# A recurrent attention kernel: the next mask matmul behind the token AV, one PSUM pool, later gates in the MLP, and w1 in three loads

**Chip, cores, metric.** One core of one Trainium2 chip. The metric is the device time of one execution in microseconds (us).

## The reference

The output is `g * a + (1 - g) * b`. Here `a` is an attention over 64 segments of 32 tokens that carries 8 memory rows from each segment to the next, and `b` is an MLP. Cut to what matters:

```python
def _A_ref(x, mem0, Wq, Wk, Wv, Wo, seg_len):      # S = 2048, Dm = 512, H = 32, Dh = 128, M = 8, seg = 32
    mem = mem0
    for s in range(n_seg):
        h = concat([mem, x[:, s*seg:(s+1)*seg]])      # 40 rows
        q, k, v = h @ Wq, h @ Wk, h @ Wv
        p = softmax(where(mask, q @ k.T * scale, -1e9))
        o = (p @ v) @ Wo
        mem = o[:, :M]                                # what the next segment waits for
        outs.append(o[:, M:])
def _B_ref(x, w1, b1, w2, b2):                     # F = 1376
    return gelu(layernorm(x) @ w1 + b1) @ w2 + b2
g = sigmoid((x * gate_w).sum(-1, keepdims=True))
```

## The kernel before

The MLP runs first, then the loop over the segments, called iterations below. The token outputs of a segment are finished one iteration late (`av_x(s - 1)`); the memory rows cannot wait. The eight PSUM banks go by number: 0 to 4 rotate, 5 and 6 serve the filling work (`run_fill`: matmuls that other segments need), and bank 7 (`B`) holds the scores, the mask, later the sums `sr`, and the next memory rows `aT`. Names used below: AV is the matmul of the probabilities with V; `wsb` is the bf16 copy that ScalarE makes (casts) of the result of Wo; the memory matmul (`mem_out`) picks the memory rows out of `wsb`; `hT` is the transposed input of the next iteration, which waits for these rows.

```python
    mps = mlp.enter_context(tc.tile_pool(name="mps", bufs=1, space=PSUM))          # MLP: tp, hp, bp
    pools = {"ps": mlp.enter_context(tc.tile_pool(name="pre", bufs=1, space=PSUM)), "sb": mwork}
    ...
    nc.sync.dma_start(w1_sb[:, :, 0:3 * P], w1_src[:, :, 0:3 * P])
    ...                                             # x rows of tiles 2 and 3, first part of w2
    nc.sync.dma_start(w1_sb[:, :, 3 * P:F], w1_src[:, :, 3 * P:F])
    ...                                             # rest of w2, then x rows of tiles 4 to 7
    def mask_mm():
        B = bank(7, [P, 512])                       # four matmuls of 448 columns into bank 7
        ...
    mlp.close()                                     # end of the MLP: its pools close
    pb = loop.enter_context(tc.tile_pool(name="pb", bufs=1, space=PSUM))           # the loop's pool
    S_next = mask_mm()
    for s in range(nseg):
        T, si = divmod(s, SPT)                      # SPT = 4: si = s mod 4
        ...                                         # q, k, v, scores, exp, memory AV
        sums(sr, E[:, :, 16:48], True, False)       # sr lies in bank 7
        ...
        nc.vector.reciprocal(out=R[:, 8 * NG:].rearrange("p (i q) -> p i q", q=32), in_=sr)
        run_fill(1)
        for u in range(8):
            wo_unit(wp, UTT[Tp % 2], 24 - 8 * sp, u)           # 8 x 4 matmuls with Wo
        nc.scalar.copy(out=wsb[:], in_=wp[:])                  # the cast of wsb
        S_next = mask_mm()
        if s >= 1:
            av_x(s - 1, (nd, ne, na, nc_))                     # token AV: 40 matmuls
        run_fill(2 * (si == 3))
        if s + 1 < nseg:
            mem_out(aT, wsb)                                   # the memory matmul, 16 pieces
            nc.vector.tensor_copy(out=hn[:, :, 0:M], in_=aT)   # hT of the next iteration
        for _ in fill:
            pass
```

## Time and profile before

| | before |
|---|---|
| time, median of 4 runs | 820.96 us (820.43 to 822.13) |
| span of the profiled run | 820.2 us |
| head (loads), MLP, loop | 0 to 25, 25 to 99.5, 100 to 820 us |
| period of an iteration, median by s mod 4 = 0, 1, 2, 3 | 10.96, 10.77, 10.94, 11.44 us |
| idle TensorE at 12.57, 17.93, 25.05, 100.62 us | 1.36, 0.63, 1.52, 0.78 us |

Such a page is read from the top: the shares say which engine to look at, the chain says whether that engine is what the end waits for, and the timeline of one iteration says what it pauses for. Below, "from the last Wo" means: counted from the start of the last four of the 32 Wo matmuls of an iteration. This is the clock by which iterations are compared, and it comes from the trace's records of single instructions, which the views merge.

### The profile page before, as it was taken

Reading aid. Unit: us, or ns where it says so; the run is one execution under the profiler, and the core shown is the slowest. Engines: PE = TensorE matmul, PEld = TensorE weight load, DVE = VectorE, ACT = ScalarE, POOL = GpSimd, SP = SyncE. Lnnn points to the kernel's source line nnn. Section 1 sums busy time; section 2 is a strip of 40 time slices with the busy share of each in tenths; the row PEclk is TensorE's granted clock in tenths of the full one; section 3 lists DMA queues with packets and bytes.
Section 4 is the critical chain, followed back from the end, with each engine's and each line's share of the span. In section 5 each row is a group of like instructions: output and inputs, shape, how many; then the busy total and the mean of one; then the engine's idle time right before and its main releaser. Section 6 shows DMA issues by size and latency. Waiting matters only on the chain.

```text
span 820.2 us, 48440 instructions
## 1 busy us (share of the span) xinstructions
PE 791.7 (97%) x22013; PEld 443.6 (54%) x22013; DVE 473.6 (58%) x897; ACT 461.8 (56%) x1365; POOL 271.4 (33%) x623
## 2 busy tenths in 40 slices
PE   5999999999999999999999999999999999999986
PEld 3666555555555555555555555555555555555543
DVE  5764256565656656665656565656656565656554
ACT  3555455656565565555555655555655556565553
POOL 8100234242434243243424242433333242424220
PEclk9999999999999999999999999999999999999999
DMA  8791310000000010101010100000010101010000
GB/s 313 241 404 48 104 34 6 25 15 17 24 22 24 14 33 10 37 11 35 5 38 9 31 16 22 25 19 28 10 36 11 36 7 38 5 34 8 10 5 24
DMA packets 38357, 37.59 MB, mean 46 GB/s; under 512 B 13561, under 2 KB 36578, under 8 KB 36610
## 3 DMA queue, kind: packets, MB, share of 16 engines
q1 hardware_dynamic: 38018, 34.31, 12.5%
q8 instruction: 174, 2.85, 1.4%
q14 instruction: 37, 0.30, 0.1%
q0 software_dynamic: 128, 0.13, 0.1%
HBM read 26.03 MB, written 6.29 MB: 39 GB/s over the span
## 4 chain that ended last, share of the span: by engine, by line
PE 93%; DVE 2%; DMA 1%; SPq 1%; issue 1%; ACT 1%; DVEq 0%; ACTq 0%
PE b L211 34%; PE b L233 17%; PE b L222 17%; PE b L398 5%; PE hp L470 4%; PE bp L487 4%; PE b L360 3%; PE b L374 2%; PE b L383 2%; PE b L365 2%; PE b L403 1%; DMA Wo_sb<-in_A_x_dram 1%; PE b L387 0%; DVE R L692 0%; DVE hT L721 0%
## 5 line engine op out<-in xcount | busy, mean ns | idle before, releaser
L217 DVE STREAM_TRANSPOSE Tt<-b 128x512 f32<-128x512 f32 (+1 forms) x384 | 225.5, 613 | 78.9 <-PE b L211 67.0
L211 PEld LDWEIGHTS <-hT 128*32 128x32 bf16 x5120 | 131.3, 97 | 109.3 <-DVE hT L721 24.7
L233 PE MATMUL b<-Wo_sb,UTT 128*32 128x512 bf16 (+1 forms) x2656 | 160.9, 378 | 0.4
L222 PE MATMUL b<-Wv_sb,hT 128*32 128x512 bf16 x2048 | 141.8, 378 | 0.0
L704 DVE RECIPROCAL R<-b 128x256 f32<-128x256 f32 x63 | 110.7, 1757 | 49.3 <-ACT UTT L703 46.8
L211 PE MATMUL b<-Wq_sb,hT 128*32 128x512 bf16 x2048 | 133.3, 380 | 3.3 <-DVE hT L721 1.7
L211 PE MATMUL b<-Wk_sb,hT 128*32 128x256 bf16 (+1 forms) x3072 | 133.3, 308 | 0.0
L667 ACT CAST KT<-Tt 128x256 bf16<-128x256 f32 (+1 forms) x192 | 87.0, 476 | 53.3 <-DVE Tt L217 53.2
L620 POOL TENSOR_TENSOR Px<-E,R 128x256 bf16<-128x256 bf16 x63 | 42.5, 675 | 209.7 <-DVE R L704 209.7
L667 POOL CAST QT<-Tt 128x512 bf16<-128x512 f32 x64 | 39.1, 611 | 187.9 <-DVE Tt L217 187.9
L233 PEld LDWEIGHTS <-UTT 128*32 128x32 bf16 x2656 | 64.8, 96 | 61.2 <-ACT UTT L703 11.1
L711 ACT CAST wsb<-b 128x512 bf16<-128x512 f32 x63 | 36.9, 585 | 97.7 <-PE b L233 97.7
L634 ACT CAST UTT<-b 128x256 bf16<-128x256 f32 x248 | 74.5, 387 | 12.2 <-PE b L403 7.9
L692 DVE RECIPROCAL R<-b 128x64 f32<-128x64 f32 x63 | 35.1, 557 | 79.8 <-PE b L360 79.8
L667 ACT CAST QT<-Tt 128x512 bf16<-128x512 f32 x64 | 39.6, 619 | 66.1 <-DVE Tt L217 66.1
L703 ACT CAST UTT<-b 128x64 bf16<-128x64 f32 x252 | 35.3, 227 | 63.1 <-PE b L403 63.1
L222 PEld LDWEIGHTS <-hT 128*32 128x32 bf16 x2048 | 49.4, 96 | 21.2
L475 ACT ACTIVATE hg<-hp,b_sb 128x256 bf16<-128x256 f32 x80 | 37.7, 473 | 39.4 <-PE hp L470 39.4
L398 PEld LDWEIGHTS <-V 32*128 32x128 bf16 x4064 | 34.4, 91 | 45.0 <-DVE Pm L695 31.7
L721 DVE CAST hT<-b 128x32 bf16<-128x32 f32 x63 | 12.0, 191 | 79.8 <-PE b L365 79.8
L470 PE MATMUL hp<-yT,w_sb 128*128 128x256 bf16 (+1 forms) x352 | 53.8, 278 | 3.4 <-ACT hg L475 1.5
L622 POOL TENSOR_TENSOR racc<-racc,R 128x320 f32<-128x320 f32 x63 | 54.7, 868 | 0.0
(130 smaller groups left out, 1032.2 us busy)
## 6 DMA issues: line engine op xcount, KB each, us to landing
Wv_sb<-in_A_Wv_dram SPq DMA_DIRECT2D x4, 1024.0 KB
Wq_sb<-in_A_Wq_dram SPq DMA_DIRECT2D x4, 1024.0 KB
Wk_sb<-in_A_Wk_dram SPq DMA_DIRECT2D x4, 1024.0 KB
Wo_sb<-in_A_Wo_dram SPq DMA_DIRECT2D x2, 2048.0 KB
vd<-vt SPq DMA_DIRECT2D x32, 128.0 KB
vs<-vd SPq DMA_DIRECT2D x256, 16.0 KB
out_dram<-o SPq DMA_DIRECT2D x15, 128.0 KB
Wo_sb<-in_A_x_dram SPq DMA_DIRECT2D x1, 1024.0 KB
```

The source lines that it names most:

```text
L211: nc.tensor.matmul(bk[32 * j:32 * j + 32, 0:n], lhsT=G[:, kc, :], rhs=W5[t][:, kc, h0:h1, j, :], start=(kc == 0), stop=(kc == KC - 1), til ...
L217: nc.vector.transpose(out=Tt[:, 0:n], in_=bk[:, 0:n])
L222: nc.tensor.matmul(bk[32 * j:32 * j + 32, :], lhsT=G[:, kc, :], rhs=Wv5[:, kc, 4 * vb:4 * vb + 4, j, :], start=(kc == 0), stop=(kc == KC - ...
L233: nc.tensor.matmul(bk[32 * g:32 * g + 32, :], lhsT=ut[:, i, j, c0:c0 + 32], rhs=Wo_sb[:, 4 * i + j, d0:d1], start=(j == 0 and i < 4), stop ...
L398: nc.tensor.matmul(U[j][:, i, :], lhsT=V[q, i, :], rhs=Pt[q, i, c_main:c_main + n], start=(i == 0), stop=False, skip_group_check=True, til ...
L470: nc.tensor.matmul(hp[:rows, :], lhsT=w1_sb[:, kc, fc * P:fc * P + rows], rhs=yTs[blk][:, kc, :], start=(kc == 0), stop=(kc == KC - 1))
L475: nc.scalar.activation(out=hg_[:rows, :], in_=hp[:rows, :], func=ACTF.Gelu_apprx_tanh, bias=b1_sb[:rows, fc:fc + 1], scale=1.0)
L620: nc.gpsimd.tensor_tensor(out=Px[:, :, 0:32], in0=E[:, :, 16:48], in1=Rr, op=ALU.mult)
L622: nc.gpsimd.tensor_tensor(out=racc[:], in0=racc[:], in1=R[:], op=ALU.add)
L634: nc.scalar.copy(out=UTT[T % 2][:, :, j, c0 + M:c0 + 40], in_=U[:])
L667: (nc.gpsimd.tensor_copy if bi == 2 else nc.scalar.copy)(out=dst, in_=Tv)
L704: nc.vector.reciprocal(out=R[:, 8 * NG:].rearrange("p (i q) -> p i q", q=32), in_=sr)
```

## The change

The intent: the mask matmul writes bank 7, which the reciprocal still reads, so it should not stand first in TensorE's queue. A single PSUM pool removes the handover of banks between the MLP and the loop. Norms (the layernorm of rows of x) should not stand behind gates (the sums for `g`) on VectorE, and w1 should arrive in smaller pieces.

```diff
+    pb = loop.enter_context(tc.tile_pool(name="pb", bufs=1, space=PSUM))     # ahead of the MLP
-    mps = mlp.enter_context(tc.tile_pool(name="mps", bufs=1, space=PSUM))
...
-    nc.sync.dma_start(w1_sb[:, :, 3 * P:F], w1_src[:, :, 3 * P:F])
+    nc.sync.dma_start(w1_sb[:, :, 3 * P:6 * P], w1_src[:, :, 3 * P:6 * P])
+    nc.sync.dma_start(w1_sb[:, :, 6 * P:F], w1_src[:, :, 6 * P:F])
...
-        tp = mps.tile([P, KC, P], BF16, tag="tp", name="tp")
+        tp = bank(k, [P, KC, P], BF16)               # k = 7; 6 for the second transpose
-        hp = mps.tile([P, TB * P], FP32, tag="hp", bufs=2, name="hp")
+        hp = bank(u % 2, [P, TB * P])
-                bpt[T] = mps.tile([P, Dm], FP32, tag=f"bp{T % 4}", name="bp")
+                bpt[T] = bank((2, 3, 4, 6)[T % 4], [P, Dm])
...
-        elif fc in (2, 4, 6, 8):
-            T = T1 + (fc - 2) // 2
+        elif fc >= 7:
+            T = T1 + fc - 7
...                                                   # (other gates likewise)
-        S_next = mask_mm()
         if s >= 1:
             av_x(s - 1, (nd, ne, na, nc_))
         run_fill(2 * (si == 3))
+        S_next = mask_mm()
```

More of the change, by code (lines that the diff above doesn't have):

```diff
@@ L93 @@
     warm = mlpw.tile([P, 1], FP32)
-    mps = mlp.enter_context(tc.tile_pool(name="mps", bufs=1, space=PSUM))
-    pools = {"ps": mlp.enter_context(tc.tile_pool(name="pre", bufs=1, space=PSUM)), "sb": mwork}
+    pools = {"sb": mwork}
     man = tc.manual_schedule()
@@ L178, in bank @@
     def bank(k, shape, dtype=FP32):
-        return pools["ps"].tile(shape, dtype, tag=f"b{k}", name=f"b{k}")
+        return pb.tile(shape, dtype, tag=f"b{k}", name=f"b{k}")
     side_n, side_todo = [0], set()
@@ L453, in norm, with norm_tr @@
         return y_sb
-    def norm_tr(T, y_sb):
+    def norm_tr(T, y_sb, k=7):
         blk, tt = divmod(T, TB)
-        tp = mps.tile([P, KC, P], BF16, tag="tp", name="tp")
+        tp = bank(k, [P, KC, P], BF16)
         for kc in range(KC):
@@ L534 @@
     norm_tr(0, ys[0])
-    norm_tr(1, ys[1])
+    norm_tr(1, ys[1], 6)
     bn(2)
@@ L558 @@
                 newton(T1 + 2, T1 + 6)
-        elif fc in (2, 4, 6, 8):
-            T = T1 + (fc - 2) // 2
+        elif fc >= 7:
+            T = T1 + fc - 7
             if T < NT:
                 gates(T, T + 1)
-        elif fc == 10 and T1 < NT:
-            gates2(T1, T1 + 4)
+        if blk % 2 == 0 and blk > 0 and fc == 1:
+            gates2(TB * blk, TB * blk + 4)
         if blk == 0 and fc in (9, 10):
@@ L569 @@
             gates2(0, 2)
-        if blk == 1 and fc in (1, 3):
-            gates(2 + fc // 2, 3 + fc // 2)
+        if blk == 1 and fc in (5, 6):
+            gates(fc - 3, fc - 2)
         if blk == 1 and fc == 9:
@@ L594 @@
     racc = lp.tile([P, NG * 40], FP32)
-    pb = loop.enter_context(tc.tile_pool(name="pb", bufs=1, space=PSUM))
     cw = loop.enter_context(tc.tile_pool(name="cw", bufs=2))
-    pools.update(ps=pb, sb=cw, nTt=3, nside=2)
+    pools.update(sb=cw, nTt=3, nside=2)
     man = tc.manual_schedule()
```

## The prediction

> **What bounds the kernel now.** I read the page first (engine shares, chain), then the waits, then the timeline of single iterations, and last the single records behind it.
>
> ```profile
> PE 791.7 (97%) x22013; PEld 443.6 (54%) x22013; DVE 473.6 (58%) x897; ACT 461.8 (56%) x1365; POOL 271.4 (33%) x623
> PE 93%; DVE 2%; DMA 1%; SPq 1%; issue 1%; ACT 1%; DVEq 0%; ACTq 0%
> ```
>
> TensorE is busy 97% of the span and holds 93% of the chain that ended last; no other engine passes 58%. The kernel has three stages: a head that waits for loads (0 to 25 us), an MLP (25 to 99.5 us, in which TensorE shows no idle piece at all in the timeline), and 64 recurrent iterations of some 11 us each (100 to 820 us). What TensorE has to do is the same in both kernels, so only its pauses can be gained. The loop is 88% of the time, so its pauses count most. Here is the end of one iteration whose number s has s mod 4 = 2, and of the next, with s mod 4 = 3:
>
> ```profile
> 307.35 1.76 DVE L704 RECIPROCAL R<-b 128x256 f32<-128x256 f32 x1 [0.66 <-ACT UTT L703]
> 309.16 0.37 PE L374 MATMUL b<-MkA,ident 128*32 128x448 bf16 x4
> 309.26 0.58 ACT L711 CAST wsb<-b 128x512 bf16<-128x512 f32 x1 [1.67 <-PE b L233]
> 309.90 0.27 PE L365 MATMUL b<-Sel,wsb 128*32 128x8 bf16 x16
> ...
> 318.39 1.76 DVE L704 RECIPROCAL R<-b 128x256 f32<-128x256 f32 x1 [0.98 <-ACT UTT L703]
> 320.20 0.37 PE L374 MATMUL b<-MkA,ident 128*32 128x448 bf16 x4
> 320.31 0.58 ACT L711 CAST wsb<-b 128x512 bf16<-128x512 f32 x1 [1.67 <-PE b L233]
> 320.51 0.37 PE L398 MATMUL b<-Px,V 32*128 32x32 bf16 x32
> 320.89 0.61 PE L233 MATMUL b<-Wo_sb,UTT 128*32 128x512 bf16 x8
> 321.34 0.26 PE L365 MATMUL b<-Sel,wsb 128*32 128x8 bf16 x16
> ```
>
> Two things are to be seen. First, the mask matmul (L374) starts 0.05 us after the reciprocal (L704) ends, both times: it writes bank 7, which the reciprocal is reading, and so it waits. In the single records this is 53 to 55 ns in all 63 iterations that have it. Second, what the next iteration waits for is the memory matmul (L365). In the first iteration it starts at 309.90, and the cast of wsb (L711) ends at 309.26 + 0.58 = 309.84; in the single records L365 starts 53 or 54 ns after the end of that cast in all iterations but those with s mod 4 = 3 (and in s = 3). With s mod 4 = 3 the cast ended at 320.89 and L365 came only at 321.34, because eight more matmuls (L233, the filling work) stand before it.
>
> **What the Trainium skill says.** "PSUM — Partial Sum Buffer", section "PSUM bank collisions raise a hardware error", gives the rule to guard PSUM by bank, not by address. The trace agrees: the mask matmul waits for a reader of its bank until 53 ns after its end. "TensorE: Matmul & The Clock Gate", section "Wait — 56ns, not 53.3ns?", gives 215.7 ns from start to start for 512 columns on a warm array; the records show 0.216 us for each four of the L233 matmuls (four column tiles side by side). "TensorEngine Tiling (Array Packing)", section "Key Properties", says that a change of the tiling mode drains TensorE. The records show 0.306 us from a mask matmul (128x32 tiles) to the first L398 (32x128 tiles), where 448 columns alone would take some 0.19. The change keeps the number of such switches. "DMA: Bandwidth & Descriptors", section "Why small descriptors are slow (HBM only)", tells of a fixed cost of each packet and descriptor; the trace's packets are used below.
>
> **Part 1, the mask matmul behind the token AV (loop).** Nothing is added or removed on TensorE; the mask goes behind 40 AV matmuls, and where there is filling work, behind that too. Times from the start of the last four Wo matmuls, from single records of before:
> - s mod 4 = 3, before: mask at 0.327 (it could have gone at 0.216, had the bank been free), first AV at 0.632, last AV at 0.908, filling work 0.109 later, two times 0.216 for it, L365 at 1.458.
> - The same, after: first AV at about 0.333 (0.306 plus 27 ns for 64 more columns), last AV 0.276 later (0.609), filling work at 0.718, end of it at 1.150, mask 0.19, L365 at about 1.34. The gain is 0.12 us.
> - 13 such iterations (11, 15, ... 59), and s = 7 with one four of filling work (1.244 before, 1.12 after): 14 x 0.12 = **1.7 us**. The way from L365 to the next iteration (sum, cast hT, first L211: 0.6 us) is unchanged and on the path, so this gain stays.
> - The other iterations, before: L365 at 1.069, which is 0.431 to the start of the cast, 0.585 of the cast, 0.053 to L365. After: last AV 0.609, mode switch 0.16, mask 0.19, so TensorE is ready for L365 at 0.96. The cast still ends last, at 1.069. **Gain 0** in 49 iterations: TensorE waits 0.11 us in front of L365 in place of the wait in front of the mask.
>
> **Part 2, one PSUM pool.** Before, the loop's pool takes over banks of pools that close, and its first mask matmul waits for the last readers of them:
>
> ```profile
> 99.25 0.60 PE L487 MATMUL bp<-w_sb,hgl 97*128 97x512 bf16 x2
> 99.88 0.69 ACT L495 ACTIVATE c_all<-bp,omg_all 128x512 bf16<-128x512 f32 x1 [0.83 <-PE bp L487]
> 100.62 0.37 PE L374 MATMUL b<-MkA,ident 128*32 128x448 bf16 x4 [0.78 <-ACT c_all L495]
> ```
>
> The listing of the instructions' order, built for both, shows that the two waits before this matmul (on VectorE and on ScalarE) are gone. Its bank 7 was last used for a transpose in block 6, and the first banks of the loop (0 to 3) were freed earlier; bank 4, which the last c_all reads, comes fifth. TensorE then goes on at about 99.7 instead of 100.62: **0.9 us**. ScalarE still has c_all (to 100.57) and a table load of 1.28 us to do, so the first QT cast can start at 102.1, where 101.9 would be wanted; the pauses of ScalarE between the next casts (0.57 us) take that up.
>
> **Part 3, w1 in three loads, and a second bank for the first transposes (head).**
>
> ```profile
> 12.57 0.61 PE L470 MATMUL hp<-yT,w_sb 128*128 128x256 bf16 x4 [1.36 <-DMA w_sb<-in_B_w_dram]
> 16.34 0.69 DVE L413 BATCH_NORM_STATS2 st<-Wo_sb 128x6 f32<-128x512 bf16 x1 [3.36 <-DMA Wo_sb<-in_A_x_dram]
> 17.93 0.38 PE L459 MATMUL tp<-ident,y 128*128 128x128 bf16 x4 [0.63 <-DVE yT L460]
> 24.43 0.20 ACT L441 ACTIVATE th_all<-z_all 128x2 f32<-128x2 f32 x1 [2.50 <-DVE junk L438]
> 25.05 0.60 PE L470 MATMUL hp<-yT,w_sb 128*128 128x256 bf16 x4 [1.52 <-ACT hg L475]
> ```
>
> The wait of 1.36 us at 12.57 goes, and the first L470 comes 0.68 us earlier (at 6.24 to 7.34 the second yT copy waits for the second use of one bank). But VectorE stands idle 3.36 us for the x rows of tiles 4 to 7, which land at 16.3 behind all of w1 and w2, and from there runs without a pause (statistics, Newton steps, two gates) until the tanh at 24.43 frees ScalarE and TensorE. TensorE's early start ends in a longer wait at the transpose of 17.93 and at 25.05. So the head gains nothing, and the third load costs: the DMA's packet records give 82 ns for 1984 bytes (512 packets on 16 engines: 2.6 us), and 45 ns for 768 bytes and some 56 ns for 1216 (estimated between 49 at 1024 and 82 at 1984): 1.4 + 1.8 = 3.2 us; by medians 0.3 us more instead of 0.6. Estimate: **0.4 us lost**.
>
> **Part 4, gates of the MLP later in odd blocks.** Fourteen gate passes (0.75 us of VectorE each) move behind norms and transposes. TensorE shows no idle piece between 25.65 and 100.6 us, so there is nothing to win: **0 us**. The tanh that waits for them moves to the second step of the even block, about 4.3 us (five steps of 0.87) after the first of four gates, which take 3 us: no new wait expected.
>
> **Sum.** 821.4 - 1.7 - 0.9 + 0.4 = 819.2 us.
>
> **The rivals.** (a) The mask's wait is on the path in all iterations: 63 times 0.12 to 0.3 us (the waits view has 15.2 us of idle weight loads at L374, 63 times), which gives 802 to 814. Against it: the 53 ns from the wsb cast to L365. (b) The head gains what it no longer waits for, 1.4 to 2 us: about 817. Against it: the idle VectorE at 16.34. (c) New waits: a tanh in front of a gelu that has to wait for late gates, or an array that has cooled in a pause of 3 us near 15 to 18; each up to 1 us, about 820.5 to 821.5. (d) Single stalls move: iterations 9, 14 and 47 of before are 0.5 us longer than their like for no cause that the trace names, and half of those with s mod 4 = 0 are 0.13 longer. A shifted stream may lose or gain some 1.5 us.
>
> **Range and chances.** My sum is -2.2; (b) and (d) stretch it to -4.7, (c) and (d) to about 0, and before itself spread 1.7 us over three runs. So 816.8 to 821.8. Two per cent is 16 us: only (a) at its most would reach it, and I give it 1%; slower by 2% has no mechanism here, 1%.
>
> **What would show it.** L374 in the loop no longer starts at the reciprocal's end; L365 still starts 53 ns after the cast of wsb except with s mod 4 = 3, where the period falls from 11.44 to 11.32 us; the others stay at 10.77 to 10.95. The first mask matmul follows L487 at once. The wait at 12.57 is gone and that at 17.93 is longer, with 25.05 at 25.3 to 25.6. It is wrong if L365 comes earlier with s mod 4 below 3, if the end of the MLP moves by more than 0.7 us, or if TensorE shows new pauses between 25 and 99 us.

## The result, and the profile after

The changed kernel takes 816.83 us (median of 4 runs, 816.19 to 818.16) against 820.96 us. The ratio is 0.995, 95% interval 0.9932 to 0.9968. This is the same within 2%, and at the lowest edge of the range of 816.8 to 821.8: the forecast gain was 2.2 us (from 821.4, the median of the runs of before that the author then had), and the measured one is about 4.1.

The page of the kernel after shows the same bound:

```profile
PE 788.6 (97%) x22013; PEld 437.1 (54%) x22013; DVE 474.9 (58%) x897; ACT 455.7 (56%) x1365; POOL 272.0 (33%) x623
PE 93%; DVE 2%; DMA 1%; SPq 1%; ACT 1%; issue 1%; DVEq 0%; ACTq 0%
```

The loop, in the timeline of the kernel after: the same two iterations as in the prediction (line numbers have moved: L376 is the mask, L367 the memory matmul, L705 the reciprocal, L712 the cast of wsb, L400 the AV, L235 the filling work):

```profile
304.81 1.76 DVE L705 RECIPROCAL R<-b 128x256 f32<-128x256 f32 x1 [0.66 <-ACT UTT L704]
306.60 0.37 PE L400 MATMUL b<-Px,V 32*128 32x32 bf16 x32
306.71 0.58 ACT L712 CAST wsb<-b 128x512 bf16<-128x512 f32 x1 [1.67 <-PE b L235]
306.98 0.37 PE L376 MATMUL b<-MkA,ident 128*32 128x448 bf16 x4
307.35 0.27 PE L367 MATMUL b<-Sel,wsb 128*32 128x8 bf16 x16
...
317.75 0.59 ACT L712 CAST wsb<-b 128x512 bf16<-128x512 f32 x1 [1.67 <-PE b L235]
318.02 0.61 PE L235 MATMUL b<-Wo_sb,UTT 128*32 128x512 bf16 x8
318.46 0.36 PE L376 MATMUL b<-MkA,ident 128*32 128x448 bf16 x4
318.65 0.25 PE L367 MATMUL b<-Sel,wsb 128*32 128x8 bf16 x16
```

The mask no longer meets the reciprocal, which ended at 306.57. With s mod 4 = 2 the memory matmul starts at 307.35, still just behind the end of the cast of wsb (306.71 + 0.58 = 307.29). With s mod 4 = 3 it comes 0.90 us after the start of the cast, where it came 1.03 us after it before (320.31 to 321.34).

The waits view shows the exchange. First a line of it for the kernel before, then one for the kernel after (waiter, releaser, us in total, times, longest):

```profile
PEld L374 <- issue: 15.2, 63, 0.3
```

```profile
PEld L367 <- ACT wsb L712: 13.9, 50, 0.6
```

63 pauses of weight loads in front of the mask became 50 pauses in front of the memory matmul.

The way from the MLP to the loop, in the timeline of the kernel after:

```profile
99.24 0.60 PE L489 MATMUL b<-w_sb,hgl 97*128 97x512 bf16 x2
99.77 0.37 PE L376 MATMUL b<-MkA,ident 128*32 128x448 bf16 x4
99.87 0.69 ACT L497 ACTIVATE c_all<-b,omg_all 128x512 bf16<-128x512 f32 x1 [0.83 <-PE b L489]
```

The mask matmul is at 99.77 instead of 100.62, ahead of the c_all (the MLP's share of the output, written by ScalarE) it used to wait for. And the head, in the same timeline:

```profile
10.91 0.61 PE L472 MATMUL b<-yT,w_sb 128*128 128x256 bf16 x4 [0.30 <-DMA w_sb<-in_B_w_dram]
16.29 0.69 DVE L415 BATCH_NORM_STATS2 st<-Wo_sb 128x6 f32<-128x512 bf16 x1 [3.63 <-DMA Wo_sb<-in_A_x_dram]
17.89 0.38 PE L461 MATMUL b<-ident,y 128*128 128x128 bf16 x4 [1.78 <-DVE yT L462]
25.04 0.60 PE L472 MATMUL b<-yT,w_sb 128*128 128x256 bf16 x4 [1.56 <-ACT hg L477]
```

The wait for w1 fell from 1.36 to 0.30 us, the one near 17.9 grew from 0.63 to 1.78, and the piece at 25.05 us is at 25.04. One pair of profiles says little of the head, though: over all 14 profiles VectorE takes up the x rows (the line at 16.29) at 15.75 to 16.34 us in the six with w1 in two loads (mean 16.06) and at 16.11 to 16.46 in the eight with three (mean 16.21).

Where the 3.8 us between the two profiled spans (820.2 and 816.4) came from, by periods and single records of these two profiles:

| part | predicted | measured |
|---|---|---|
| 14 iterations with s mod 4 = 3 and filling work, from the last Wo to the next q | -1.7 | -1.8 |
| 16 iterations with s mod 4 = 0, the same stretch | 0 | **-1.3** |
| the other iterations, and the stretch from q to the last Wo (single stalls that come and go) | 0 | +0.3 |
| MLP to loop | -0.9 | -0.8 |
| head | **+0.4** | 0.0 |
| after the loop | 0 | -0.1 |

The +0.3 is a sum of -0.9 and +1.2: single stalls of up to 0.7 us fell in other places. The -1.3 us was not predicted, and the experiments had to find its cause. In the kernel before, 8 of the 16 iterations with s mod 4 = 0 take 0.13 to 0.22 us longer from the last Wo to hT than the rest. In the changed kernel's first profile none does.

### The profile page after: what moved, and what is told of

Its sections match the earlier page's. It is cut to its first block, busy times and chain, and to the rows that moved or that the text cites. A ratio compares the mean times of both kernels' runs of the same rounds, so it can differ in the third digit from the quotient of the medians.

```text
span 816.4 us, 48441 instructions
## 1 busy us (share of the span) xinstructions
PE 788.6 (97%) x22013; PEld 437.1 (54%) x22013; DVE 474.9 (58%) x897; ACT 455.7 (56%) x1365; POOL 272.0 (33%) x623
## 4 chain that ended last, share of the span: by engine, by line
PE 93%; DVE 2%; DMA 1%; SPq 1%; ACT 1%; issue 1%; DVEq 0%; ACTq 0%
PE b L213 34%; PE b L235 17%; PE b L224 16%; PE b L400 5%; PE b L472 4%; PE b L489 4%; PE b L362 3%; PE b L376 2%; PE b L367 2%; PE b L385 2%; PE b L405 1%; DMA Wo_sb<-in_A_x_dram 1%; PE b L389 0%; DVE hT L722 0%; PE b L322 0%
## 5 line engine op out<-in xcount | busy, mean ns | idle before, releaser
L235 PE MATMUL b<-Wo_sb,UTT 128*32 128x512 bf16 (+1 forms) x2656 | 161.8, 378 | 0.4
L705 DVE RECIPROCAL R<-b 128x256 f32<-128x256 f32 x63 | 110.7, 1758 | 49.2 <-ACT UTT L704 48.4
L235 PEld LDWEIGHTS <-UTT 128*32 128x32 bf16 x2656 | 64.8, 96 | 61.1 <-ACT UTT L704 11.1
L712 ACT CAST wsb<-b 128x512 bf16<-128x512 f32 x63 | 36.9, 585 | 97.7 <-PE b L235 97.7
L400 PEld LDWEIGHTS <-V 32*128 32x128 bf16 x4064 | 34.4, 91 | 59.4 <-DVE Pm L696 32.2
L477 ACT ACTIVATE hg<-b,b_sb 128x256 bf16<-128x256 f32 x80 | 37.7, 473 | 39.3 <-PE b L472 39.3
L472 PE MATMUL b<-yT,w_sb 128*128 128x256 bf16 (+1 forms) x352 | 53.8, 278 | 2.4 <-ACT hg L477 1.6
```

The source lines that it names most:

```text
L235: nc.tensor.matmul(bk[32 * g:32 * g + 32, :], lhsT=ut[:, i, j, c0:c0 + 32], rhs=Wo_sb[:, 4 * i + j, d0:d1], start=(j == 0 and i < 4), stop ...
L400: nc.tensor.matmul(U[j][:, i, :], lhsT=V[q, i, :], rhs=Pt[q, i, c_main:c_main + n], start=(i == 0), stop=False, skip_group_check=True, til ...
L472: nc.tensor.matmul(hp[:rows, :], lhsT=w1_sb[:, kc, fc * P:fc * P + rows], rhs=yTs[blk][:, kc, :], start=(kc == 0), stop=(kc == KC - 1))
L477: nc.scalar.activation(out=hg_[:rows, :], in_=hp[:rows, :], func=ACTF.Gelu_apprx_tanh, bias=b1_sb[:rows, fc:fc + 1], scale=1.0)
```

## The experiments

Twelve runs, in three calls; those of one call ran on one chip and share the runs of the kernel before (medians 820.67, 820.67 and 820.40 us).

**e1_mask: the first part alone.**

```diff
-        S_next = mask_mm()
         if s >= 1:
             av_x(s - 1, (nd, ne, na, nc_))
         run_fill(2 * (si == 3))
+        S_next = mask_mm()
```

> The kernel before with only the mask matmul moved behind the token AV and the filling work. My theory: the memory matmul L365 comes 0.13 us earlier in the 14 iterations with s mod 4 = 3 that have filling work, nothing in the other 49: -1.8 us. Where the profile of the change also lost stalls of 0.14 us in about 9 iterations with s mod 4 = 0: if the order of mask and AV is their cause, they are gone here too and the sum is -3.1 us; if they are chance, they are here as often as before. Rival (the mask's wait is on the path in all 63): -7 us or more.

Measured: 817.72 us, 2.95 us below before, ratio 0.9964 (0.9951 to 0.9978). The memory matmul came at 1.327 us (median) with s mod 4 = 3 and at 1.069 in the others, as predicted. With s mod 4 = 0, one iteration of 16 was long. So the order of mask and AV carries both the 1.8 us and the 1.2 us, and the rival of 7 us or more falls.

**e2_pool: the second part alone** (the pool lines and bank numbers of the diff above, nothing else).

> The kernel before with only the one PSUM pool (banks of the MLP by number, a second bank for the first two transposes). Theory: the first mask matmul of the loop comes 0.85 us earlier, right after the last MLP matmul, and the loop keeps its periods (11.44 us for s mod 4 = 3): -0.85 us. The stalls of 0.14 us with s mod 4 = 0 are here if they belong to the old order of mask and AV. Rival: the gain of 0.85 us is lost behind the table load of ScalarE: 0.

Measured: 819.79 us, 0.9 us below before, ratio 0.9992 (0.9978 to 1.0005), an interval that still holds 1. Its timeline shows no idle piece in front of the first mask matmul any more, the period with s mod 4 = 3 is 11.44 us, and 9 of the 16 iterations with s mod 4 = 0 are long.

**e3_head: the third and fourth parts alone** (w1 in three loads, gates later).

> The kernel before with only the MLP's later gates and w1 in three loads. Theory: the wait of 1.36 us for w1 near 12.6 us shrinks or goes, but the wait near 18 us grows by as much, and the TensorE piece at 25.05 us stays where it is within 0.1 us: 0 us. Rival: the head is bound by w1, then -1 us or more; second rival: more packets make the x rows land later, then +0.3 to +0.6 us.

Measured: 820.96 us, ratio 1.0004 (0.999 to 1.0017). The wait for w1 is gone from its timeline, the wait near 17.7 us is 0.74 us and that at 24.82 us is 1.50. No gain and no loss that these runs can tell; the interval holds the expected 0 and the second rival's +0.3 to +0.6 alike. Long iterations with s mod 4 = 0 are there.

**e4_after: the changed kernel again.**

> The changed kernel again, for a second profile and more rounds: -4 us against before (ratio 0.995). The profile tells whether the stalls with s mod 4 = 0 are absent again (theory: yes, the order of mask and AV removes them) or come and go (rival: chance, then some of the 16 iterations show 0.14 us more).

Measured: 816.33 us, ratio 0.9952 (0.9939 to 0.9966). The three parts measured alone sum to -2.95 - 0.9 + 0.3 = -3.6 us, beside -4.3 for all of it; a difference of 0.7 us is within what such medians scatter (a repeat below moved by about 1 us). Two of its 16 iterations with s mod 4 = 0 were long, so the new order makes them rare, not impossible.

**e6_fill1: one unit of filling work in front of the mask** (on the changed kernel).

```diff
-        run_fill(2 * (si == 3))
+        run_fill(si == 3)
```

> The changed kernel with one unit of filling work instead of two ahead of the mask matmul with s mod 4 = 3. Theory: there the memory matmul L367 waits for TensorE's own work, and the period follows it. It comes at 1.12 us instead of 1.33 us after the last four Wo matmuls, the second unit fits into the 0.25 us in which TensorE waits for hT, and 13 iterations lose 0.22 us each: -2.8 us against the changed kernel, so some 813.5 us. Rival (the period of these iterations is set elsewhere, as by ScalarE's casts): 0.

Measured: 814.61 us, ratio 0.9927 (0.9914 to 0.9941). The median period with s mod 4 = 3 fell from 11.31 to 11.10 us, as expected. By the medians the gain was only 1.7 us, so it was run again (e11).

**e7_before_dummy and e9_after_dummy: the same extra work in both orders.** Four matmuls of 224 columns (0.093 us) that write part of the mask twice, put into `mask_mm` of the kernel before and of the changed one.

```diff
+        for j in range(4):
+            q = slice(32 * j, 32 * j + 32)
+            nc.tensor.matmul(S[q, 0:4, :], lhsT=ident[:, q], rhs=MkA[:, 0:2, :].unsqueeze(2).to_broadcast([P, 2, 2, EW]), ...)
         for j in range(4):
```

> The kernel before with four more matmuls of 224 columns (0.093 us) in front of the mask matmul; they write part of the mask a second time, so the result is right. Theory: in the old order TensorE is ready for L365 just when the cast of wsb ends (1.068 and 1.069 us), so every added 0.093 us shows in all 63 iterations: +5.8 us. Rival (in the 49 iterations the old order had slack too): +1.3 us.

> The changed kernel with the same four added matmuls of 224 columns (0.093 us) in front of the mask matmul. Theory: in the new order TensorE has 0.11 us of slack in front of L367 in 49 iterations, so the added work shows only in the 14 with s mod 4 = 3 that have filling work: +1.3 us against the changed kernel, some 817.7 us. Rival (the wait for the wsb cast is not what L367 waits for): +5.8 us.

Measured: in the old order 825.75 us, +5.1 us where 5.8 was expected; in the new order 817.77 us, +1.4 us over the 816.33 that the changed kernel took (e4). The ratios to before of the same rounds, 0.9965 and 0.9952, put it at 1.1 us. The timelines say why. Old order:

```profile
309.01 0.38 PE L378 MATMUL b<-MkA,ident 128*32 128x448 bf16 x4
309.01 0.59 ACT L715 CAST wsb<-b 128x512 bf16<-128x512 f32 x1 [1.66 <-PE b L233]
309.32 0.37 PE L402 MATMUL b<-Px,V 32*128 32x32 bf16 x32
309.70 0.26 PE L365 MATMUL b<-Sel,wsb 128*32 128x8 bf16 x16
```

New order:

```profile
306.47 0.59 ACT L716 CAST wsb<-b 128x512 bf16<-128x512 f32 x1 [1.66 <-PE b L235]
306.73 0.28 PE L376 MATMUL b<-MkA,ident 128*32 128x224 bf16 x4
307.11 0.26 PE L367 MATMUL b<-Sel,wsb 128*32 128x8 bf16 x16
```

In the old order the memory matmul now starts 0.10 us after the end of the cast (309.60), behind TensorE's own AV. In the new one it still starts 0.05 us after it (307.06). The same work costs 0.1 us an iteration in one order and nothing, with s mod 4 below 3, in the other. So after the change TensorE does have slack there, and the cast of wsb is what the memory matmul waits for. One thing more is to be seen in the old order: with s mod 4 = 1 or 2 the added work moves the start of the memory matmul by only 0.04 to 0.05 us, but hT by the whole 0.09. So that start alone did not set when hT came in the old order; e8 shows what else did.

**e8_tr: the DMA transposes of x one iteration later** (on the kernel before). These are loads of x that transpose on the way; SyncE issues them.

```diff
-        if si == 1 and T + 2 < NT:
+        if si == 2 and T + 2 < NT:
             x_load(T + 2)
```

> The kernel before with the DMA transposes of x issued one iteration later in the program (s mod 4 = 2 instead of 1). In the old order some 8 to 10 of the 16 iterations with s mod 4 = 0 are 0.14 us longer, just those in which a DMA transpose is issued 0.86 to 0.93 us after the last four Wo matmuls, while the token AV runs. Theory (the issue of a transpose during the AV delays the AV): these delays go, -1.2 us, and come back only where a transpose now meets an AV. Rival (they belong to something else of these iterations, such as the filling work): no change in them, 0 us.

Measured: 819.69 us, 1.0 us below before, ratio 0.9988 (0.9975 to 1.0002). The sum by time alone would be weak, but the profile is clear: of the 15 iterations with s mod 4 = 0 that have a token AV, one is long, and none has a transpose in that stretch. Four transposes now fall into the same stretch of iterations with s mod 4 = 1, and two of these are long. A long one of the kernel before (s = 16; SPq is the queue of SyncE, which issues the transposes, the second of them at 287.63 by the single records):

```profile
286.48 3.08 SPq L241 DMA_TRANSPOSE xT<-in_A_x_dram  x2
287.39 0.37 PE L398 MATMUL b<-Px,V 32*128 32x32 bf16 x32
288.12 1.20 ACT L634 CAST UTT<-b 128x256 bf16<-128x256 f32 x4 [0.34 <-PE b L365]
288.32 0.19 DVE L721 CAST hT<-b 128x32 bf16<-128x32 f32 x1 [1.29 <-PE b L365]
```

The same iteration of e8_tr, with no transpose near it:

```profile
286.18 0.37 PE L398 MATMUL b<-Px,V 32*128 32x32 bf16 x32
286.76 1.20 ACT L634 CAST UTT<-b 128x256 bf16<-128x256 f32 x4 [0.19 <-PE b L403]
286.96 0.19 DVE L721 CAST hT<-b 128x32 bf16<-128x32 f32 x1 [1.14 <-PE b L365]
```

From the AV's start to the first cast of its result it is 0.73 us with the transpose and 0.58 without, and hT comes later by the same 0.15 us. The changed kernel with a transpose issued at the same place (s = 24; the second at 373.83):

```profile
372.67 4.31 SPq L243 DMA_TRANSPOSE xT<-in_A_x_dram  x3
373.26 0.37 PE L400 MATMUL b<-Px,V 32*128 32x32 bf16 x32
373.86 1.21 ACT L635 CAST UTT<-b 128x256 bf16<-128x256 f32 x4
374.36 0.19 DVE L722 CAST hT<-b 128x32 bf16<-128x32 f32 x1 [1.14 <-PE b L367]
```

Here the AV is over before the transpose is issued, and nothing is late.

What is late in a long iteration is not the start of any matmul. In the single records of the kernel before, the AV and the memory matmul start at the same times in long and short ones (to 5 ns from the last Wo). Late are the signals by which TensorE reports that matmuls are done (its semaphore updates, which the packed trace holds and the views do not print). In short iterations the AV's last signal comes 0.163 us after the start of the memory matmul, in the long ones 0.305 (median; in seven of the eight, while in the eighth only the memory matmul's own signal is late). The memory matmul's signal, for which hT waits, follows that of the AV by 0.159 us in the short ones and in those seven.

In the new order the AV's last signal comes 0.157 us ahead of the start of the memory matmul, and the two signals are 0.475 us apart. So the old order had no room between them, and the new one has 0.3 us. The room is what counts: in the seven profiles of the new order ten iterations with s mod 4 = 0 have AV signals that are 0.06 to 0.13 us late, all with a transpose recorded some 1.2 to 1.3 us after the last Wo, and hT is on time in all ten. In the five long iterations of the new order, counted below, the memory matmul's own signal is late.

Counted over the profiles (iterations with s mod 4 = 0 and s > 0; long means hT begins over 1.48 us after the last Wo):

| | a transpose issued 0.6 to 1.1 us after the last Wo | none there |
|---|---|---|
| old order: before, e2, e3, e13 | 31 of 32 long | 4 of 28 long |
| new order: changed kernel three times, e1, e6, e9, e11 | 5 of 52 long | 0 of 53 long |

The stretch of 0.6 to 1.1 us was chosen with the profiles in view. Of the four long ones without a transpose in it, two (e3 and e13, s = 4) have one shortly after it, at about 1.2 us. Left out are e7, where added work makes every iteration long, and e8 and e12, where the transposes were moved.

**e10_after, e11_fill1, e12_fill1_tr, e13_before_fill1: what is left, compared on one chip.** e10 is the changed kernel, e11 is e6 again, e12 adds the later transposes of e8 to it, and e13 has e6's edit on the kernel before.

> The changed kernel a third time, beside the two that follow, so that they are compared with it on one chip: ratio to before 0.995, some 816.3 to 816.8 us. Its iterations with s mod 4 = 0 are at their short length (hT 1.41 us after the last four Wo matmuls) but for one or two.

> The changed kernel with one unit of filling work ahead of the mask, again. The first run gave periods 0.213 us shorter in 13 iterations (2.8 us) but a median only 1.7 us lower, with the changed kernel run in another call. If the 2.8 us are real, it is 2.8 us below the changed kernel of this call; if something gives back 1 us, 1.7 us.

> The changed kernel with one unit of filling work and with the DMA transposes of x one iteration later. Theory: in the new order the token AV is over before the transposes are issued, so moving them gains next to nothing here: within 0.5 us of the run before it. Rival (transposes cost in both orders): -1 us.

> The kernel before with one unit of filling work instead of two with s mod 4 = 3. Theory: L365 comes at 1.24 us instead of 1.46 us there, 13 iterations lose 0.2 us each: -2.7 us against before, so this gain does not need the change; the mask's wait still costs 0.13 us in each of them.

Measured: e10 816.61 us; e11 813.36 us (ratio to before 0.9909, 0.9894 to 0.9924); e12 813.51 us (0.9913, 0.99 to 0.9927); e13 818.67 us (0.998, 0.9966 to 0.9994). e11 is 3.25 us below e10, so the 2.8 us are real and the 1.7 of the first try was scatter of about 1 us. The later transposes add nothing in the new order (e12 beside e11), as the theory has it. e13 gained 1.7 us where 2.7 was expected. Its period with s mod 4 = 3 fell from 11.44 to 11.23 us, which is 13 x 0.215 = 2.8 us; the missing 1 us is as large as the scatter just named, and these runs do not decide what it is. The timeline of e11 shows how the filling unit found its place:

```profile
316.68 0.59 ACT L712 CAST wsb<-b 128x512 bf16<-128x512 f32 x1 [1.67 <-PE b L235]
316.94 0.40 PE L235 MATMUL b<-Wo_sb,UTT 128*32 128x512 bf16 x4
317.17 0.36 PE L376 MATMUL b<-MkA,ident 128*32 128x448 bf16 x4
317.36 0.26 PE L367 MATMUL b<-Sel,wsb 128*32 128x8 bf16 x16
```

The memory matmul starts 0.68 us after the start of the cast instead of 0.90, and the other unit lies behind it, while TensorE would wait for hT anyway. e11, with e12 beside it within the noise, is the best of the kernels run, 7 us below before.

## Why the prediction came out as it did

- **Part 1, s mod 4 = 3: right.** 14 x 0.12 us was predicted; the records give 1.83 us over these 14 iterations, and L367 at 1.328 us where 1.34 was worked out.
- **Part 1, the other 49: the mechanism was right, the zero was not.** The memory matmul does wait for the cast of wsb (1.069 us before and after, and e7 beside e9), so taking the mask's wait away gains nothing there by itself. The step that failed is "Gain 0 in 49 iterations": it looked only at the start of the memory matmul. Moving the AV 0.32 us forward also put room between its signals and that of the memory matmul, which DMA transposes make late in half of the iterations with s mod 4 = 0. The prediction had seen these 0.13 us stalls, but filed them under rival (d) as stalls that move by chance "for no cause that the trace names". They had a cause that the trace names, if the issue times on SyncE's queue are laid beside them. That term was -1.3 us in the profiles, and e1 and e8 show it on the two sides: move the AV, or move the transposes. A smaller slip: the 0.16 us of the mode switch (last AV to memory matmul) was itself a wait for the cast. From the last AV to the mask it is 0.11 in the new order, and in e7, where the cast ends earlier, 0.11 to the memory matmul. So TensorE is ready some 0.18 us before the memory matmul starts, in place of 0.11, and in the old order it was ready 0.05 us before, not just when the cast of wsb ends, as the expectation of e7 has it.
- **Part 2: right.** 0.9 us predicted, 0.85 in the trace (100.62 to 99.77), and 0.9 by the times of e2.
- **Part 3: the mechanism was right, and the 0.4 us loss is not shown.** Rival (b) falls: the load of the x rows is on the chain that ended last in both kernels, and TensorE's gain of 1.06 us at 12.57 became a longer wait at 17.89. The doubtful term is the cost of the third load. Its packets did take longer in sum, much as estimated (means of 41 ns for 768 bytes and 54 ns for 1216 give 1.3 + 1.7 = 3.0 us against 2.6). In the pair of profiles nothing came later for it: the last packet of w1 ended at 12.02 us in place of 12.15, and the x rows were used at 16.29 in place of 16.34. Over all profiles they were used 0.15 us later with three loads, which is less than the 0.6 us by which profiles with two loads differ. So a loss anywhere from 0 to 0.4 us stays possible.
- **Part 4: right** as far as tested. No idle piece of TensorE appears between 25.04 and 99.77 us. It was run only together with the loads (e3).
- **Rival (a)** falls with e1 and e9. **Rival (c)** did not occur: the windows view gives a granted clock of 1.00 for 15 to 20, 20 to 25 and 25 to 30 us in both kernels.

The 1.3 us of gain that was missed, and a loss of 0.4 that this pair of profiles does not show, point the same way, so the time came out at the edge of the range.

What stays open: how a DMA transpose makes TensorE's signals late by some 0.15 us. The runs show that the loss takes both, the transposes and signals without room. The recorded issue time is only a mark of it: in the new order the late AV signals come before it. The four long iterations of the old order without a transpose in the stretch, and the single stalls of 0.4 to 0.7 us (iterations 9, 14 and 47 before; 14, 22, 45 and 47 after), have no cause that these traces name.

## What to carry to other kernels

A wait that is removed gains only where nothing else ends later, and whether that is so can be tested: put the same small extra work into both versions, and the one with slack does not show it (here 1.1 to 1.4 us beside 5.1). An instruction that starts on time can still report late: look at what its reader waits for, not at its start alone. A stall that comes in half of some iterations should not be called chance before the issue times of all queues, the DMA's above all, have been laid beside it. When reordering has freed time in front of a critical instruction, look at what else stands there: moving one unit of filling work behind it was worth another 3 us.

## What the Trainium skill lacked or had wrong

- No page that was read has it: a DMA transpose issued about when a group of small row-tiled matmuls (32x128 tiles) runs comes with signals of TensorE that are some 0.15 us late, though no matmul starts later: 31 of 32 such iterations of the old order are long, against 5 of 52 where the group stands earlier. It would belong to "DMA: Bandwidth & Descriptors", section "DMA Transpose (X-bar)".
- "TensorEngine Tiling (Array Packing)", section "Key Properties", says that a change of the tiling mode drains TensorE but gives no cost. The records show 0.306 us from four 448-column matmuls to the first AV matmul in the other mode, where 448 columns take about 0.19 (an estimate: 0.216 us, the records' spacing for 512 columns, times 448/512), so some 0.12 us for this switch.
- "DMA: Bandwidth & Descriptors", section "Why small descriptors are slow (HBM only)", tells of a fixed cost of each packet, but not of what it costs the load behind. Here 0.4 us more of packet time for the same bytes (992 KB in rows of 768 and 1216 bytes instead of 1984) goes with x rows that are used 0.15 us later on the mean (16.21 beside 16.06 us, eight and six profiles), within their spread.
